# A float32 gated linear-attention block on one core: the split of a reloaded weight tile put late in the key/value stage, and an early gate/up quarter moved to other PSUM banks with the last key/value product ordered behind it

## The chip, the core and the metric

The kernel runs on one core of a Trainium2 chip. A core has five engines with a queue of their own each: TensorE (PE in the profile, PEld for its weight loads), VectorE (DVE), ScalarE (ACT), GpSimd (POOL) and SyncE (SP), which here only issues DMAs. Each engine takes its instructions in the order in which the program lists them, and waits at an instruction until the semaphores that it names have been raised. The metric is device time in microseconds of one execution; the comparison is between medians of repeated executions.

## The reference, cut to what matters

```python
xn = _layernorm(x)                       # x: 1 x 2048 x 576
qkv = xn @ wqkv                          # 32 heads of 18
phi_k = [softmax(k @ w_phi), softmax(-k @ w_phi)]     # per head, 36 features
kv = einsum("bhsf,bhsd->bhfd", phi_k, v)
z  = einsum("bhsf->bhf", phi_k)
o  = (phi_q @ kv) / (phi_q @ z + 1e-6)   # phi_q made of q as phi_k of k
s  = o @ wo
g  = silu((silu(xn @ w_gate) * (xn @ w_up)) @ w_down) # hidden width 4608
out = x + s * g
```

The sums `kv` and `z` run over all 2048 rows, so no row's attention output can be formed before the last key/value row is added.

## The kernel before, in words

All of it is float32. A product in the fast format of TensorE (float32r) is made of three: each operand is split into a rounded part `hi` (a cast on ACT) and the rest `lo` (a subtraction on DVE or POOL), and hi·hi, hi·lo and lo·hi are added in PSUM. `split_rows` (L61) is such a split for a weight tile of the gated branch: one cast on ACT (L62) and two subtractions on DVE (L63, L64).

The program is written with a tile framework. It gives every tile a buffer of its pool, places the waits, and puts the instructions in an order of its own; blocks under `tc.high_priority()` come first among what is ready, and `tc.issue_after(ins)` puts those instructions of a block that run on `ins`'s engine behind `ins` in that engine's queue, and leaves the block's other engines alone.

The stages in order of time:

1. Until about 71 us the rows are normalized, transposed and split (`XB`), weights of keys, queries and values are split, and early tiles of the gated branch run between. An early tile (`early_tile`, L111) is one of the first `EARLY` = 6 blocks of 128 hidden columns of gate and up, made for one half of the rows (`i`) and one block of 512 rows (`j`): 14 matmuls into a gate bank `pg`, Silu on ACT (L117), 14 matmuls into an up bank `pu`, their product on DVE (L120), stored to DRAM. Its weights come from `early_weights(f)` (L99): two tiles `raw` by DMA (L105), each split into `wh` and `wl`. `raw` has two buffers, `wh` and `wl` three. The tiles of f = 0 and f = 1 run for one half of the rows here; for the other half the weights of f = 0 are loaded a second time (L621), and those of f = 1 are kept.
2. From about 71 to 240 us, the key/value stage: eight pairs of 128-row tiles. `k_tile` (L398) makes the keys' features: 28 matmuls into the two-bank PSUM tile `p2` (shown as `p`), per-head maximum and minimum and their subtraction on DVE (L275, L276), Exp on ACT (L279), the sums, reciprocal and scaling on DVE (L282, L283, L406). The values go to the banks `vx`, `vy`, `vw`: two plain products a tile in the first two pairs, and from the third pair on seven products for two tiles (a Strassen-like scheme), whose operands `shi` and `slo` are sums of rows that POOL makes a pair ahead (L308 to L325, the cast of L323 on ACT). Values are copied to the tiles `v0`, `v1` by ACT (L391) or added by DVE (L396). `kv_step` (L286) then adds phi^T·v of one tile into the three banks `kvp`, ten products, for one tile while the next tile is made; the step of the last tile, `kv_step(*pend)` (L486), stands after the loop. In the trace each of the ten is two passes, so a `kv_step` shows 20 matmuls: eight for `kvp0`, eight for `kvp1`, four for `kvp2`.
3. After the loop a quarter of an early tile (f = 1, i = 0, j = 0) runs in the bank pair `p2` (L485), and the sums are turned around: `z` is copied (`zc`, L497), spread over all partitions by small matmuls (L503) and copied to `zb` (L506); each block of `kv` is masked (`km`, L510, DVE) and split (`KVH`, `KVL`).
4. From 240 to about 555 us the queries, their features, the numerators and the projection with `wo` (`WOH`, `WOL`, loaded by L528 through one buffer `ez`), with the other early tiles between.
5. From 555 us to the end the other 30 hidden blocks of gate and up, and the product with `w_down`.

The change touches `early_weights`, `early_tile`, `xw` (which issues the 14 matmuls, L92), the loop of pairs, what stands behind it, and L621.

Of the kernel before, what the change touches and what calls it, by code (L numbers as in the profile page):

```python
# [9 lines left out]
F32 = mybir.dt.float32  # L10
# [6 lines left out]
S, D, H, DH, F = 2048, 576, 32, 18, 4608  # L17
P = 128
NT = S // P
BT = 512  # L20
# [5 lines left out]
GW = GH * DH  # L26
# [20 lines left out]
def gated_hedgehog_kernel(ctx: ExitStack, tc, x, w_qk, w_v, w_phi, wo, w_gu, w_tail, w_down, ident_in, mask_in, out):  # L47
# [5 lines left out]
    nc = tc.nc  # L53
# [7 lines left out]
    def split_rows(hi, lo, src):  # L61
        nc.scalar.copy(hi, src)  # L62
        nc.vector.tensor_sub(lo, src[:, :, 0:2], hi[:, :, 0:2])  # L63
        nc.vector.tensor_sub(hi[64:96, :, 2], src[64:96, :, 2], hi[64:96, :, 2])  # L64
# [17 lines left out]
    def xw(ps, i, j, cols, wh, wl, stationary_x):  # L82
        pairs = []
        for k in range(2):
            b = XB[i][2 * j + k]
            for c in range(2):
                pairs += [(b[:, c, cols], w[:, k, c]) for w in (wh, wl)]
                pairs += [(b[:, 3 + c, cols], wh[:, k, c])]
            pairs += [(b[0:96, 2, cols], wh[0:96, k, 2])]
        for n, (a, b) in enumerate(pairs):  # L90
            l, r = (a, b) if stationary_x else (b, a)
            nc.tensor.matmul(ps, l, r, start=n == 0, stop=n == len(pairs) - 1)  # L92

    est = ctx.enter_context(ExitStack())
    epool = est.enter_context(tc.tile_pool(name="epool", bufs=2, side="right"))
    pes = ctx.enter_context(ExitStack())
    eps = pes.enter_context(tc.tile_pool(name="eps", bufs=2, space=PSUM, side="right"))

    def early_weights(f):  # L99
        parts = []  # L100
        for m in (0, 2):
            raw = epool.tile([P, 2, 3, P], F32, name="raw", bufs=2)
            hi = epool.tile([P, 2, 3, P], F32R, name="wh", bufs=3)
            lo = epool.tile([P, 2, 2, P], F32R, name="wl", bufs=3)
            nc.sync.dma_start(raw, w_gu[f, :, m:m + 2])  # L105
            with tc.high_priority():
                split_rows(hi, lo, raw)
            parts.append((hi, lo))
        return parts

    def early_tile(f, i, parts, js=(0, 1), banks=None):  # L111
        for j in js:
            pg, pu = banks or [eps.tile([P, BT], F32, name="pe") for _ in range(2)]
            xw(pg, i, j, slice(0, BT), *parts[0], False)
            h = epool.tile([P, BT], F32, name="h")
            with tc.high_priority():
                nc.scalar.activation(h, pg, AF.Silu)  # L117
            xw(pu, i, j, slice(0, BT), *parts[1], False)
            with tc.high_priority():
                nc.vector.tensor_mul(h, pu, h)  # L120
            nc.sync.dma_start(h_dram[i, f, :, j * BT:(j + 1) * BT], h)

    with ExitStack() as att:
        const = att.enter_context(tc.tile_pool(name="const", bufs=1))
# [8 lines left out]
        with ExitStack() as wst:  # L133
# [259 lines left out]
            def v_add(v, ps):  # L393
                with tc.high_priority():
                    for d, src in v_parts(v, ps, 0):
                        nc.vector.tensor_add(d, src, d)  # L396

            def k_tile(t):  # L398
# [7 lines left out]
                nc.vector.tensor_mul(heads(phi), heads(phi), spread(sm, 2 * H))  # L406
                return phi

            bank = [0]
# [15 lines left out]
            for p in range(8):  # L425
# [59 lines left out]
            early_tile(1, 0, first_weights[1], (0,), [spare[:, n] for n in range(2)])  # L485
            kv_step(*pend)  # L486

        with ExitStack():
            qc = att.enter_context(tc.tile_pool(name="qc", bufs=1, reuse_waits="tile"))
# [7 lines left out]
                    nc.scalar.copy(zc[0:w, 4 * i + j:4 * i + j + 1], kvp[i][0:w, j, w:w + 1])  # L497
            for a, m in ((0, 4), (4, 1)):
                o, w = GROUPS[a]
                for s in range(2):  # L500
                    zp = kps.tile([P, 512], F32, name=("vx", "vy")[s] if a == 0 else ("vw", "p2")[s])
                    for g in range(a, a + m):
                        nc.tensor.matmul(zp[:, (g - a) * GW:(g - a) * GW + w],  # L503
                                         zc[0:w, 2 * g + s:2 * g + s + 1].to_broadcast([w, P]), ident[0:w, 0:w],
                                         start=True, stop=True)
                    nc.scalar.copy(zb[:, s * D + o:s * D + o + m * w], zp[:, 0:m * w])  # L506
            for i in range(2 * NG):
                o, w = GROUPS[i // 2]
                km = qc.tile([GW, GW], F32, name="km", bufs=2)
# [549 lines left out]
```

## Time and profile before

| | us |
|---|---|
| median of 3 runs (lowest, highest) | 1649.32 (1647.87, 1653.42) |
| the profiled execution | 1654.06 |
| its span, first to last instruction | 1652.2 |
| PE busy | 1611.5 (98%) |
| DVE busy | 1179.7 (71%) |
| ACT busy | 726.7 (44%) |
| POOL busy | 657.0 (40%) |

The views used below: a table of stretches gives the busy time of each engine between two times, and the clock that TensorE was granted (1.00 is full); a timeline lists instructions by their start, with their duration, and in brackets the idle time of the engine before them and what ended it; the chain of waits follows the work that ended last back from the end, here in order of time with start and duration. All times count from the first instruction. A TensorE matmul's shown duration includes its way through the array, so matmuls in a row start closer together than they last.

### The profile page before, as it was taken

The numbers are of one execution on the slowest core, as the hardware profiler recorded it, in microseconds if no ns is written. First come the engines' busy times: TensorE is split into PE (matmuls) and PEld (weight loads), VectorE is DVE, ScalarE is ACT, GpSimd is POOL, SyncE is SP. The second block draws the span as 40 slices with busy tenths as digits, with TensorE's granted clock in tenths as the row PEclk, the third lists the DMA queues.
The fourth block names the chain that finished last, engine by engine and source line by source line (L and its number), as shares of the span: only waits on it lengthen the run. The fifth ranks groups of instructions, "written<-read, shape, count | busy, mean of one in ns | idle before, by whom it ended". The sixth has DMA issues, their size and how long they took to land.

```text
span 1652.2 us, 25252 instructions
## 1 busy us (share of the span) xinstructions
PE 1611.5 (98%) x9399; PEld 1434.4 (87%) x9399; DVE 1179.7 (71%) x1731; ACT 726.7 (44%) x1407; POOL 657.0 (40%) x695
## 2 busy tenths in 40 slices
PE   6989999999999999999999999999999999999997
PEld 5889988899987788888888888888888888888886
DVE  7667767988972376887887777844666677566578
ACT  5533345444452365444445445445433333333334
POOL 3476662233302354554564453422333244133132
PEclk9999999999999999999999999999999999999999
DMA  8522234244317645455455554495545556555434
GB/s 286 200 88 78 77 117 130 79 127 122 90 50 247 236 167 173 170 175 185 160 180 177 174 177 164 134 361 174 167 123 161 174 168 214 155 183 184 139 114 172
DMA packets 121276, 266.46 MB, mean 161 GB/s; under 512 B 12770, under 2 KB 52834, under 8 KB 119362
## 3 DMA queue, kind: packets, MB, share of 16 engines
q1 hardware_dynamic: 106188, 244.49, 45.0%
q0 software_dynamic: 3072, 11.02, 2.5%
q10 hardware_dynamic: 11894, 9.35, 1.8%
q8 instruction: 74, 1.21, 0.3%
q14 instruction: 48, 0.39, 0.1%
HBM read 165.98 MB, written 98.83 MB: 160 GB/s over the span
## 4 chain that ended last, share of the span: by engine, by line
PE 91%; DVE 3%; DMA 2%; issue 1%; ACT 1%; POOL 1%; SPq 0%; ACTq 0%; POOLq 0%; DVEq 0%
PE pd L787 24%; PE px L688 23%; PE pw L688 11%; PE pe L92 7%; PE p L92 7%; PE py L688 6%; PE p L598 4%; PE kvp L292 2%; PE po L584 2%; PE vx L380 1%; PE pt L578 1%; PE vw L380 1%; PE tp L218 1%; DMA xn<-in_A_x 0%; DVE acc L759 0%
## 5 line engine op out<-in xcount | busy, mean ns | idle before, releaser
L787 PEld LDWEIGHTS pd<-dw,hh 128*128 128x128 f32 x3048 | 431.8, 188 | 25.2 <-DVE dw L59 2.2
L787 PE MATMUL pd<-dw,hh 128*128 128x288 f32 x3048 | 447.8, 297 | 3.2 <-DVE dw L59 1.5
L688 PE MATMUL px<-X,w 128*128 128x512 f32 x1440 | 373.5, 393 | 1.8 <-ACT w L58 1.0
L688 PEld LDWEIGHTS px<-X,w 128*128 128x128 f32 x1440 | 261.4, 188 | 53.2 <-ACT s L717 3.9
L688 PE MATMUL pw<-X,w 128*128 128x512 f32 x720 | 185.6, 393 | 0.0
L688 PEld LDWEIGHTS pw<-X,w 128*128 128x128 f32 x720 | 134.7, 189 | 30.4 <-DVE s L722 0.3
L912 DVE TENSOR_TENSOR acc<-pd,acc 128x576 f32<-128x576 f32 x128 | 96.1, 752 | 80.1 <-PE pd L787 80.0
L722 DVE TENSOR_TENSOR s<-pw,s 128x512 f32<-128x512 f32 x120 | 82.5, 687 | 97.7 <-ACT s L717 86.8
L92 PE MATMUL pe<-X,wh 128*128 128x512 f32 (+1 forms) x460 | 144.6, 399 | 1.9 <-POOL X L200 0.7
L717 ACT COPY s<-px 128x512 f32<-128x512 f32 x120 | 70.3, 586 | 154.8 <-PE px L688 154.7
L58 ACT CAST hh<-ha 128x512 fp32r<-128x512 f32 x140 | 82.7, 619 | 95.6 <-PE pd L787 73.3
L59 DVE TENSOR_TENSOR hh<-ha,hh 128x512 fp32r<-128x512 f32 x140 | 108.6, 801 | 17.3 <-ACT hh L58 15.7
L884 POOL TENSOR_TENSOR hb<-hb 128x512 f32<-128x512 f32 x34 | 45.3, 1332 | 163.1 <-DVE hb L744 162.6
L92 PEld LDWEIGHTS pe<-X,wh 128*128 128x128 f32 (+1 forms) x460 | 84.9, 189 | 19.5 <-POOL X L200 1.1
L59 DVE TENSOR_TENSOR w<-ld,w 128x512 fp32r<-128x512 f32 (+1 forms) x90 | 77.1, 859 | 33.4 <-ACT w L58 32.3
L897 POOL TENSOR_TENSOR ha<-ha 128x512 f32<-128x512 f32 x34 | 52.6, 1564 | 109.3 <-DVE hh L59 109.3
L688 PE MATMUL px<-X,wt 96*128 96x512 f32 x240 | 94.8, 395 | 0.0
L688 PE MATMUL py<-X,w 128*128 128x512 f32 x360 | 94.0, 395 | 0.1
L58 ACT CAST w<-ld 128x512 fp32r<-128x512 f32 (+1 forms) x90 | 49.4, 549 | 85.3 <-POOL ld L678 53.7
L871 POOL TENSOR_TENSOR h<-ha,hb 128x512 f32<-128x512 f32 x34 | 45.5, 1338 | 100.8 <-DVE ha L748 66.6
L729 ACT COPY py<-px 128x512 f32<-128x512 f32 x60 | 34.3, 572 | 98.0 <-PE px L688 81.2
L688 PEld LDWEIGHTS py<-X,w 128*128 128x128 f32 x360 | 64.5, 188 | 11.8 <-ACT py L729 1.0
(254 smaller groups left out, 3250.6 us busy)
## 6 DMA issues: line engine op xcount, KB each, us to landing
w_dram<-w SPq DMA_DIRECT2D x87, 512.0 KB, 3.0
w<-w_dram SPq DMA_DIRECT2D x87, 512.0 KB, 4.3
wt<-t_dram SPq DMA_DIRECT2D x59, 336.0 KB, 3.7
ld<-in_B_w_gu SPq DMA_DIRECT2D x30, 512.0 KB
X<-sum_dram SPq DMA_DIRECT2D x8, 1280.0 KB, 10.0
rt<-in_B_w_down SPq DMA_DIRECT2D x33, 288.0 KB, 2.9
rb<-in_B_w_down SPq DMA_DIRECT2D x33, 288.0 KB, 5.9
w_dram<-w SPq DMA_DIRECT2D x29, 256.0 KB, 2.0
```

What stands on the lines that cost most here:

```text
L58: nc.scalar.copy(hi, src)
L59: nc.vector.tensor_sub(lo, src, hi)
L92: nc.tensor.matmul(ps, l, r, start=n == 0, stop=n == len(pairs) - 1)
L598: nc.tensor.matmul(ps[:, 0:HALF], a[0:w, g, jc], bw[0:w, g, n], start=k == 0, stop=k == 3 * NG - 1)
L688: nc.tensor.matmul(ps, l, r, start=first and n == 0, stop=last and n == len(mm) - 1, skip_group_check=True)
L717: nc.scalar.copy(t, ps)
L722: nc.vector.tensor_add(t, ps, t)
L787: nc.tensor.matmul(ps, l, r, start=first and n == 0 and m == 0, stop=n == len(hs) - 1 and m == 2, skip_group_check=True)
L871: sub(s, g["h"][0][0], g["h"][0][1])
L884: nc.gpsimd.tensor_add(a21, a21, g["h"][1][1])
L897: sub(a12, a12, g["h"][0][0])
L912: nc.vector.tensor_add(a2, pd[:, :, 0:HALF], a2)
```

## The change

Four edits:

- `early_weights` takes a second argument `behind`. Where it is given, the split is ordered behind that instruction. For the second load of f = 0 it is the scaling (L406 before, L411 after) of the thirteenth key tile, which `k_tile` now records in `features`. That scaling runs on DVE, so the two DVE subtractions are moved, and the ACT cast is not.
- In each pair from the third on, the `kv_step` of the pair's first tile is written ahead of the last value product (`x[3]` with weights 6) and its copy.
- The early quarter after the loop goes to the banks `vy` (gate) and `vx` (up) in place of `p2`, and the last `kv_step` is ordered behind its last matmul.
- The spread `z` goes to one two-bank tile `p2` (and `vw` for the last, narrow group) in place of `vx`, `vy`, `vw` and `p2` one by one.

```diff
-    def early_weights(f):
+    def early_weights(f, behind=None):
...
             nc.sync.dma_start(raw, w_gu[f, :, m:m + 2])
-            with tc.high_priority():
-                split_rows(hi, lo, raw)
+            with tc.issue_after(behind.ins) if behind else ExitStack():
+                with tc.high_priority():
+                    split_rows(hi, lo, raw)
...
                 sm = softmax_parts(pk, phi)
-                nc.vector.tensor_mul(heads(phi), heads(phi), spread(sm, 2 * H))
+                features.append(nc.vector.tensor_mul(heads(phi), heads(phi), spread(sm, 2 * H)))
...
                 v_add(v1, vx)
+                kv_step(2 * p, phi0, v0)
                 v_product(vx, x[3], 6, False, True)
                 v_copy(v1, vx, 1)
-                kv_step(2 * p, phi0, v0)
...
-            spare = kps.tile([P, 2, 512], F32, name="p2")
-            early_tile(1, 0, first_weights[1], (0,), [spare[:, n] for n in range(2)])
-            kv_step(*pend)
+            spare = early_tile(1, 0, first_weights[1], (0,), [kps.tile([P, BT], F32, name=n) for n in ("vy", "vx")])
+            with tc.issue_after(spare.ins):
+                kv_step(*pend)
...
             for a, m in ((0, 4), (4, 1)):
                 o, w = GROUPS[a]
+                zp = kps.tile([P, 2, 512 if a == 0 else 256], F32, name="p2" if a == 0 else "vw")
                 for s in range(2):
-                    zp = kps.tile([P, 512], F32, name=("vx", "vy")[s] if a == 0 else ("vw", "p2")[s])
...
-            parts = first_weights.pop() if f == 1 else early_weights(f)
+            parts = first_weights.pop() if f == 1 else early_weights(f, features[12] if f == 0 else None)
```

What the framework makes of it. POOL's instructions stand as before. On SP one load of `raw` (for f = 2) moves from the first pairs to the sixth, behind the moved split, since it takes that split's buffer. Line numbers after are larger by 3 to 5 (L406 is L411, L292 is L295, L380 is L383, L503 is L508).

DVE before, in the first two pairs (`p_860` is the key tile of the second tile, `p_955` of the third; `sm` the sums):

```order
L275 TENSOR_REDUCE m<-p_860 128x32
L276 TENSOR_TENSOR phi<-p_860,m 128x576
L282 TENSOR_REDUCE sm<-phi 128x64
L63 TENSOR_TENSOR wl<-raw,wh 128x512
L64 TENSOR_TENSOR wh<-raw,wh 32x2x128
L283 RECIPROCAL sm<-sm 128x64
L406 TENSOR_TENSOR phi<-phi,sm 128x1152
L275 TENSOR_REDUCE m<-p_955 128x32
```

DVE after, at the same place:

```order
L278 TENSOR_REDUCE m<-p_860 128x32
L279 TENSOR_TENSOR phi<-p_860,m 128x576
L285 TENSOR_REDUCE sm<-phi 128x64
L286 RECIPROCAL sm<-sm 128x64
L411 TENSOR_TENSOR phi<-phi,sm 128x1152
L278 TENSOR_REDUCE m<-p_955 128x32
```

DVE after, in the seventh pair (`p_1921` is the key tile of its first tile, `p_2015` of its second):

```order
L286 RECIPROCAL sm<-sm 128x64
L411 TENSOR_TENSOR phi<-phi,sm 128x1152
L63 TENSOR_TENSOR wl<-raw,wh 128x512
L64 TENSOR_TENSOR wh<-raw,wh 32x2x128
L278 TENSOR_REDUCE m<-p_2015 128x32
```

The two subtractions have left the place between the sums and the reciprocal of the second tile and stand behind the scaling of the thirteenth.

ACT before, at the end of a pair (`v_742` is `v0`, `v_743` is `v1`):

```order
L279 ACTIVATE phi<-phi 128x576
L391 COPY v_743<-vx 128x90
L391 COPY v_743<-vx 128x126
L391 COPY v_743<-vx 128x72
L279 ACTIVATE phi<-phi 128x576
L323 CAST shi<-sraw 128x768 x2
```

ACT after, at the same place:

```order
L282 ACTIVATE phi<-phi 128x576 x2
L394 COPY v_743<-vx 128x90
L394 COPY v_743<-vx 128x126
L394 COPY v_743<-vx 128x72
L326 CAST shi<-sraw 128x768 x2
```

The second Exp now stands ahead of the copies of the pair's last value product, and on PE that product follows all ten `kvp` products of the first tile instead of six of them.

PE before, at the end of the stage, the middle of the early quarter (`p_2305`) and what follows its last matmuls (two pieces):

```order
L92 MATMUL p_2305<-X_61,wh 128x512 x2
L92 MATMUL p_2305<-X_61,wl 128x512
L92 MATMUL p_2305<-X_61,wh 128x512 x2
L292 MATMUL kvp_918<-v_743,phi 126x127 x4
L292 MATMUL kvp_919<-v_743,phi 126x127 x4
L92 MATMUL p_2305<-X_60,wh 128x512
L92 MATMUL p_2305<-X_60,wl 128x512
```

```order
L292 MATMUL kvp_920<-v_743,phi 72x73 x2
L503 MATMUL vx<-ident,zc 128x126 x4
L503 MATMUL vy<-ident,zc 128x126 x4
L503 MATMUL vw<-ident,zc 128x72
L503 MATMUL p_2382<-ident,zc 128x72
L92 MATMUL p_2482<-QH,X_64 128x288
```

PE after, from the end of the early quarter (now in `vy` and `vx`) to the first query tile (`p_2481`):

```order
L92 MATMUL vx<-X_61,wl 128x512
L92 MATMUL vx<-X_61,wh 128x512 x2
L295 MATMUL kvp_918<-v_743,phi 126x127 x4
L295 MATMUL kvp_919<-v_743,phi 126x127 x4
L295 MATMUL kvp_920<-v_743,phi 72x73 x2
L508 MATMUL p_2368<-ident,zc 128x126 x4
L508 MATMUL vw<-ident,zc 128x72
L508 MATMUL p_2368<-ident,zc 128x126 x4
L508 MATMUL vw<-ident,zc 128x72
L92 MATMUL p_2481<-QH,X_64 128x288
```

The last tile's ten products stood between the gate and the up half of the quarter, with the last two behind the up half; now all stand behind the whole quarter. The second group of spread `z` follows the first in the same tile.

More of the change, by code (lines that the diff above doesn't have):

```diff
@@ L91, in xw @@
             l, r = (a, b) if stationary_x else (b, a)
-            nc.tensor.matmul(ps, l, r, start=n == 0, stop=n == len(pairs) - 1)
+            last = nc.tensor.matmul(ps, l, r, start=n == 0, stop=n == len(pairs) - 1)
+        return last
     est = ctx.enter_context(ExitStack())
@@ L117, in early_tile @@
                 nc.scalar.activation(h, pg, AF.Silu)
-            xw(pu, i, j, slice(0, BT), *parts[1], False)
+            last = xw(pu, i, j, slice(0, BT), *parts[1], False)
             with tc.high_priority():
@@ L121, in early_tile @@
             nc.sync.dma_start(h_dram[i, f, :, j * BT:(j + 1) * BT], h)
+        return last
     with ExitStack() as att:
@@ L396, in v_add @@
                         nc.vector.tensor_add(d, src, d)
+            features = []
             def k_tile(t):
@@ L499, in gated_hedgehog_kernel @@
                 o, w = GROUPS[a]
+                zp = kps.tile([P, 2, 512 if a == 0 else 256], F32, name="p2" if a == 0 else "vw")
                 for s in range(2):
-                    zp = kps.tile([P, 512], F32, name=("vx", "vy")[s] if a == 0 else ("vw", "p2")[s])
                     for g in range(a, a + m):
-                        nc.tensor.matmul(zp[:, (g - a) * GW:(g - a) * GW + w],
+                        nc.tensor.matmul(zp[:, s, (g - a) * GW:(g - a) * GW + w],
                                          zc[0:w, 2 * g + s:2 * g + s + 1].to_broadcast([w, P]), ident[0:w, 0:w],
                                          start=True, stop=True)
-                    nc.scalar.copy(zb[:, s * D + o:s * D + o + m * w], zp[:, 0:m * w])
+                    nc.scalar.copy(zb[:, s * D + o:s * D + o + m * w], zp[:, s, 0:m * w])
             for i in range(2 * NG):
```

## The prediction

> **What bounds the kernel now.** I read the page, then the waits of PE, then the chain of waits and the timelines around each place that the change touches.
>
> ```profile
> span 1652.2 us, 25252 instructions
> PE 1611.5 (98%) x9399; PEld 1434.4 (87%) x9399; DVE 1179.7 (71%) x1731; ACT 726.7 (44%) x1407; POOL 657.0 (40%) x695
> ```
>
> PE is busy all but 40.7 us of the span. The change adds no matmul and takes none away, so it can only move PE's idle time and the clock that PE gets. Time won in the key/value stage reaches the end as far as PE stays the engine that is waited for. The profiled execution took 1654.06 us, 1.86 more than its span and 4.74 more than the median of the runs, 1649.32. I work out a difference in the profile's time and take it off the median.
>
> The first place is PE's wait before the second `kv_step`. The chain of waits there (start, duration):
>
> ```profile
> 99.33 4.23 PE kvp L292 x20
> 103.56 2.75 PE vw L92 x14
> 106.31 3.73 PE p L92 x28
> ...
> 111.89 2.02 PE kvp L292 x20
> 113.91 1.92 PE vy L92 x14
> ```
>
> The same 20 passes take 4.23 us here and 2.02 one tile later; 14 value matmuls take 2.75 and 1.92. The waits of PE in this stage, and the stretches, say why:
>
> ```profile
> PE kvp L292 <- DVE phi L406: 5.4, 1, 5.4
> ```
>
> ```profile
> 99.33:103.30 3.97, 3.97 (x20) 3.97 (x21) 3.15 (x5) 1.71 (x4) 3.81 (x6) 0.50 0.47 165
> 221.97:240.00 18.03, 14.30 (x96) 12.41 (x94) 13.80 (x29) 8.90 (x32) 12.38 (x13) 1.00 0.31 103
> 229.00:240.00 11.00, 7.96 (x55) 7.05 (x55) 8.12 (x21) 3.94 (x23) 9.24 (x10) 1.00 0.40 133
> 262.31:268.00 5.69, 5.69 (x30) 5.65 (x31) 2.18 (x3) 2.75 (x4) 0.00 (x0) 0.70 0.31 96
> ```
>
> PE stood idle from 93.93 to 99.33, and then had half the clock (0.50). What held it is in the timelines of DVE, ACT and POOL:
>
> ```profile
> 87.52 1.35 DVE L282 TENSOR_REDUCE sm<-phi 128x64 f32<-128x1152 f32 x1 [1.76 <-ACT phi L279]
> 94.34 0.69 DVE L63 TENSOR_TENSOR wl<-raw,wh 128x512 fp32r<-128x512 f32 x1 [5.47 <-ACT wh L62]
> 95.04 0.92 DVE L64 TENSOR_TENSOR wh<-raw,wh 32x256 fp32r<-32x256 f32 x1
> 96.58 2.60 DVE L406 TENSOR_TENSOR phi<-phi,sm 128x1152 f32<-128x1152 f32 x1
> ```
>
> ```profile
> 86.46 0.44 ACT L391 COPY v<-vw 128x252 f32<-128x252 f32 x2
> ...
> 93.47 0.83 ACT L62 CAST wh<-raw 128x768 fp32r<-128x768 f32 x1 [5.99 <-DMA raw<-in_B_w_gu]
> ...
> 95.71 0.67 ACT L351 CAST TH<-sraw 128x576 fp32r<-128x576 f32 x1 [0.90 <-POOL sraw L348]
> 96.29 0.52 ACT L391 COPY v<-vx 128x90 f32<-128x90 f32 x3
> ```
>
> ```profile
> 93.55 0.80 POOL L347 TENSOR_TENSOR sraw<-sraw 128x288 f32<-128x288 f32 x1
> 94.43 1.25 POOL L348 TENSOR_TENSOR sraw<-sraw 128x288 f32<-128x288 f32 x1
> ```
>
> DVE finished the sums at 88.87 and then stood 5.47 us before the subtraction of the reloaded weights, because ACT's cast waited for their DMA until 93.47. The reciprocal and the scaling of the features, which PE needs, are behind it. ACT was held by the same load, and the rest of the values (`v<-vx`) were copied only at 96.29, behind a cast of `TH` that waited for POOL.
>
> **The change, part by part.**
>
> *The moved split at its old place.* With the two subtractions gone, the reciprocal follows the sums at once: 0.55 us for it and at most 2.60 for the scaling (the slowest row) bring `phi` to about 92.1, ahead of PE's 93.93. But the ACT cast stays where it was, so the second reason remains. Of the ten `kvp` products, the first four use values copied at 86.46 and can run at 93.93 (0.8 of the 2.02 us); the other six wait for `v<-vx`. That copy stood behind the `TH` cast, and this behind POOL's L348, which took 1.25 us beside DVE's subtraction where L347 took 0.80. Without the neighbour I give it 0.80, and `v<-vx` comes 0.45 earlier. PE goes on at 96.2, or at 96.9 if nothing on POOL gets faster and all three copies are awaited. The idle time left is 1.5 to 2.2 us. Six products take 1.2, the value matmuls 1.92, and the next key tile starts between 99.3 and 100.0, before 106.31. That is 6.3 to 7.0 us; I take 6.6, in the middle. The rest of the wait and the half clock are in it about equally: 3.0 are the slow rows (2.21 and 0.83).
>
> Whether PE keeps its clock over the idle time left is open. After 2.13 us of idle (the row of 239.99 below) it stayed at 1.00, after 1.94 (262.31 below) it fell, to a mean of 0.70 over 5.69 us, which is 1.7 us lost. So the low end is 6.3 less 1.7, 4.6. The Trainium skill ("TensorE: Matmul & The Clock Gate", HAM oscillation) asks only that no idle gap exceed about 3.4 us; by that rule the term would stay at 6.6 with no low end. The 1.94 us row contradicts it, and the row decides.
>
> *The moved split at its new place.* It goes ahead of the seventh pair's second key tile, where DVE waits:
>
> ```profile
> 201.94 0.76 DVE L275 TENSOR_REDUCE m<-p 128x32 f32<-128x576 f32 x1 [1.88 <-PE p L92]
> ```
>
> 0.69 and 0.92 us fit into 1.88, so it costs nothing; were the cover gone, `m` would be 1.6 us late, and the key tile behind it with its bank. The DMA of `raw` that SP now issues behind it has nothing in its queue behind it until the sums of that pair are stored, and its first reader is in the next stage. No cost.
>
> *The pair.* PE's work is the same, but the last value product ends later by the four `kvp` products ahead of it, and on ACT the copies, then the casts of the row sums for POOL, follow it. A pair before, the first two rows from the chain:
>
> ```profile
> 186.82 0.94 PE vx L380 x7
> 187.76 0.88 PE kvp L292 x8
> ```
>
> ```profile
> 187.79 0.52 ACT L391 COPY v<-vx 128x90 f32<-128x90 f32 x3 [1.70 <-PE vx L380]
> 188.19 0.71 ACT L279 ACTIVATE phi<-phi 128x576 f32<-128x576 f32 x1
> 188.78 1.58 ACT L323 CAST shi<-sraw 128x768 fp32r<-128x768 f32 x2
> ```
>
> ```profile
> 191.93 1.72 POOL L324 TENSOR_TENSOR shi<-sraw,shi 32x256 fp32r<-32x256 f32 x1
> 193.73 1.29 POOL L325 TENSOR_TENSOR slo<-sraw,shi 128x512 fp32r<-128x512 f32 x1
> ```
>
> ```profile
> 195.28 0.29 PE L380 MATMUL vx<-TH,slo 128*128 128x288 f32 x1
> ```
>
> The copies move from 187.79 to 188.67; the Exp is now ahead of them, in time that ACT had idle (1.70), so the casts start at about 189.1 in place of 188.78. POOL's last `slo` then ends near 195.3 in place of 195.02, and PE needs it at 195.28. In five pairs (the fourth to the eighth, which use sums made in such a pair) PE can lose from nothing to 0.3 us each: 0 to 1.7 in all. I take 0.7, nearer the low end since the whole shift is about the slack. There is a second effect on these rows:
>
> ```profile
> 190.91 2.15 DVE L406 TENSOR_TENSOR phi<-phi,sm 128x1152 f32<-128x1152 f32 x1
> ...
> 198.70 1.36 DVE L406 TENSOR_TENSOR phi<-phi,sm 128x1152 f32<-128x1152 f32 x1
> ```
>
> The scaling takes 2.15 beside POOL and 1.36 alone, and POOL's L324 ended just after it: they hold each other up. The Exp half a microsecond earlier puts the scaling against another POOL instruction. The Trainium skill ("SBUF — State Buffer", two separate sides) has VectorE and GpSimd take turns on a shared port pair, each for a whole instruction; by it the scaling gets in ahead of the first `slo` and the last ends near 195.5, some 0.3 a pair, and the term would be 1.4. The rows show the holding up, not the order after the change, so I keep 0.7.
>
> *The end of the stage.*
>
> ```profile
> 229.61 2.00 PE L292 MATMUL kvp<-v,phi 128*126 128x127 f32 x16 [1.29 <-DVE phi L406]
> ...
> 237.45 0.41 PE L503 MATMUL p<-ident,zc 72*128 72x72 f32 x2 [0.30 <-DVE h L120]
> 239.99 0.40 PE L92 MATMUL p<-QH,X 128*128 128x288 f32 x1 [2.13 <-ACT zb L506]
> ```
>
> From 221.97 to 239.99 PE is idle for 1.29, 0.30 and 2.13, 3.72 in all. After, the whole quarter (28 matmuls) hides the last features, so the 1.29 goes; the product on DVE (L120) is long done, so the 0.30 goes. What is late next is the spread of `z`: its second group is written to the same tile as the first, and I read it as waiting until `zb` has been copied from the first, on ACT, behind casts of `KVH` that each wait for a `km` of DVE:
>
> ```profile
> 234.03 0.50 ACT L58 CAST KVH<-km 126x126 fp32r<-126x126 f32 x2 [1.65 <-DVE km L510]
> ```
>
> That cast waited 1.65 once. Bounds for what PE waits there: 0.3, if the `zb` copy passes at once, and 2.2, one such wait and a copy of 0.5. I take 0.7, near the low end, since here DVE isn't stopped by L120 in the middle of its row. Then the query tile follows with no wait for the last copy, as it now takes other banks. Gain 3.7 less 0.7: 3.0 (1.5 to 3.4).
>
> *Behind it.* All this moves PE ahead of the loads of `wo`, which go through one buffer one by one:
>
> ```profile
> 259.23 0.68 ACT L58 CAST WOH<-ez 126x576 fp32r<-126x576 f32 x1 [3.28 <-DMA ez<-in_A_wo]
> ```
>
> ```profile
> 259.94 0.76 DVE L59 TENSOR_TENSOR WOL<-ez,WOH 126x576 fp32r<-126x576 f32 x1 [2.20 <-ACT WOH L58]
> ```
>
> ```profile
> 262.31 0.58 PE L92 MATMUL p<-QH,X 128*128 128x288 f32 x1 [1.94 <-DVE e L276]
> ```
>
> PE waits 1.94 there for a subtraction queued on DVE behind the split of the second block of `wo`. The first load is issued behind POOL's last sums, which depend on ACT's `KVH` casts and not on PE's matmuls, so it moves forward by less than PE. If none of the 3.0 reached the loads, all would be lost here; if they kept pace, nothing. I take a loss of 0.6, near the low end, because each later load is issued by the DVE row behind PE.
>
> *Sum:* 6.6 − 0.7 + 3.0 − 0.6 = 8.3 us less. 1654.06 would become 1645.8, the median 1649.32 becomes 1641.0, 0.5% faster.
>
> **The rivals.**
>
> *The end's gain is lost at `wo`.* For it: the wait exists and DVE is in order. Against: the loads follow PE for most of their way. Then 6.6 − 0.7 = 5.9, less some tenths: about 1643.7.
>
> *The key wait only changes its owner.* ACT's queue, not moved, still holds the values until 96.9, and PE's clock falls all the same: 4.6 of the first term, with the pair and `wo` at their worse ends (1.7, 1.3) and 1.5 at the end: 3.1 us, 1646.2, no difference to be told. For it: the cast of L62 stands where it stood. Against: the copy is at 96.29 already in this trace.
>
> *The clock also stays up at 262.31*, because the windows over which it is judged fall elsewhere: 1.7 more, 1639.3.
>
> *Slower.* The pair's chain PE, ACT, POOL, PE closes on itself, and each pair becomes longer by what POOL is late. It decides from 1.7 us a pair on (8.3 over five); at 2.7 it gives 1654. For it: the slack is only 0.26 (195.28 less 195.02). Against: the product moves by 0.88, so being later than that needs POOL's four instructions to slow down too; L324 at 1.72 against some 0.7 is the largest such stretch.
>
> **How the numbers follow.** Forecast 0.52, end's gain lost 0.18, clock kept at 262.31 as well 0.10, owner changed 0.13, slower 0.07. A difference under 0.3% (4.9 us) can't be told from none. The first and third are faster, and of the second two thirds: 0.75. Within: 0.18. Slower: 0.07. The range runs from 1649.3 − 12.6 (7.0, no loss in the pairs, 3.4, 1.7 at 262.31, and 0.5 for the scatter of the median) to the rival whose owner changed, with a microsecond of scatter: 1636.7 to 1647.2.
>
> **What would show it.** Right: the PE wait for `phi` before the second `kv_step` is gone, with 1 to 2.5 us behind the first four products, ended by ACT's copy (L394); a key tile near 100 in place of 106.31; pairs of 18.2 to 18.5 us; no wait for `phi` at the end, and one of under 1.5 before the second spread of `z`; the first query tile some 9 us earlier than 239.99. Wrong: a pair of 19 us or more, a new half-clock stretch before 100, or a wait above 4 us where 1.94 was.

## The result and the profile after

The changed kernel took 1646.26 us in the median of 14 executions (1644.42 to 1648.05), the kernel before 1650.54 in as many beside it: a ratio of 0.9973, with an interval of 0.9965 to 0.9982, 4.3 us less. In a second comparison it was 1646.18 against 1652.02, 0.9961 (0.9949 to 0.9974), 5.8 us less. The forecast was 8.3 us less, at 1641.0. So the sign was right and the size was not.

The profiled execution took 1644.69. Its page:

```profile
span 1642.9 us, 25249 instructions
PE 1610.5 (98%) x9399; PEld 1433.5 (87%) x9399; DVE 1176.6 (72%) x1731; ACT 727.5 (44%) x1407; POOL 653.2 (40%) x695
```

The waits of PE at the places of the change (total, times, longest):

```profile
PE p L92 <- DVE e L279: 2.7, 1, 2.7
PE p L508 <- ACT zb L511: 0.8, 1, 0.8
PE kvp L295 <- ACT v L394: 0.4, 1, 0.4
```

The waits for `phi` (5.4 and 1.3) are gone. 0.4 is left at the first place and 0.8 before the second spread of `z`, and the wait at the third query tile has grown from 1.94 to 2.7.

*The first place.* ACT's timeline, then the chain of waits:

```profile
92.87 0.84 ACT L62 CAST wh<-raw 128x768 fp32r<-128x768 f32 x1 [5.64 <-DMA raw<-in_B_w_gu]
...
95.15 0.51 ACT L394 COPY v<-vx 128x90 f32<-128x90 f32 x3
```

```profile
93.74 0.81 POOL sraw L351
...
95.43 1.40 PE kvp L295 x12
96.83 1.93 PE vw L92 x14
98.76 3.73 PE p L92 x28
```

ACT still waits for the reloaded weights, but the copies of the values come at 95.15 in place of 96.29, and PE goes on at full clock: the value matmuls take 1.93 in place of 2.75, and the next key tile starts at 98.6 in place of 106.1.

*The new place of the split.* DVE, ahead of the seventh pair's second key tile:

```profile
192.76 1.50 DVE L63 TENSOR_TENSOR wl<-raw,wh 128x512 fp32r<-128x512 f32 x1
194.28 1.14 DVE L64 TENSOR_TENSOR wh<-raw,wh 32x256 fp32r<-32x256 f32 x1
195.45 0.76 DVE L278 TENSOR_REDUCE m<-p 128x32 f32<-128x576 f32 x1
```

The two subtractions took 0.69 and 0.92 at their old place and take 1.50 and 1.14 here, beside POOL's sums: 2.64, more than the 1.88 that should have covered them. The reduction behind them has no idle time left.

*The pair.* DVE's scaling, then POOL's operands for the next pair:

```profile
165.11 1.65 DVE L411 TENSOR_TENSOR phi<-phi,sm 128x1152 f32<-128x1152 f32 x1
```

```profile
164.81 0.73 POOL L327 TENSOR_TENSOR shi<-sraw,shi 32x256 fp32r<-32x256 f32 x1 [4.75 <-ACT shi L326]
165.62 2.28 POOL L328 TENSOR_TENSOR slo<-sraw,shi 128x512 fp32r<-128x512 f32 x1
167.98 0.73 POOL L327 TENSOR_TENSOR shi<-sraw,shi 32x256 fp32r<-32x256 f32 x1
168.79 1.29 POOL L328 TENSOR_TENSOR slo<-sraw,shi 128x512 fp32r<-128x512 f32 x1
```

```profile
169.88 1.19 PE vx L383 x7
```

Before, the scaling (190.91) met the second L324 (1.72), and the first `slo` went ahead of it:

```profile
190.56 1.28 POOL L325 TENSOR_TENSOR slo<-sraw,shi 128x512 fp32r<-128x512 f32 x1
```

Now the scaling starts ahead of the first `slo`, which takes 2.28 in place of 1.28. The last `slo` ends at 170.08, inside PE's `vx` product, which takes 1.19 where seven of its kind take 0.94 elsewhere: 0.25 a pair.

*The end of the stage.* PE:

```profile
225.12 2.18 PE L295 MATMUL kvp<-v,phi 128*126 128x127 f32 x20
...
229.21 1.16 PE L508 MATMUL p<-ident,zc 126*128 126x126 f32 x8 [0.79 <-ACT zb L511]
...
230.34 0.38 PE L92 MATMUL p<-QH,X 128*128 128x288 f32 x1
```

All twenty passes of the last `kv_step` run in one piece, and the only wait left is 0.79, where 0.7 was forecast. The first query tile starts at 230.34 in place of 239.99, 9.65 us earlier.

*The loads of `wo`.* SP before, then after:

```profile
246.11 0.44 SPq L528 DMA_DIRECT2D ez<-in_A_wo  x1
249.21 0.83 SPq L535 DMA_DIRECT2D tl<-in_B_w_tail  x2
250.14 0.36 SPq L105 DMA_DIRECT2D raw<-in_B_w_gu  x1
...
253.25 0.33 SPq L105 DMA_DIRECT2D raw<-in_B_w_gu  x1
254.14 0.34 SPq L528 DMA_DIRECT2D ez<-in_A_wo  x1
```

```profile
239.38 0.44 SPq L533 DMA_DIRECT2D ez<-in_A_wo  x1
242.08 0.83 SPq L540 DMA_DIRECT2D tl<-in_B_w_tail  x2
243.02 0.36 SPq L106 DMA_DIRECT2D raw<-in_B_w_gu  x1
...
243.96 0.38 SPq L106 DMA_DIRECT2D raw<-in_B_w_gu  x1
244.44 0.42 SPq L533 DMA_DIRECT2D ez<-in_A_wo  x1
```

The first load of `wo` moved forward by 6.7 us, less than PE, and the second by 9.7, as PE did. So what stands between them closed up: the second load was issued 4.9 us behind the first load of `tl` before, and 2.4 now, with both loads of `raw` in between. What it then took, before and after (chain of waits, start and duration):

```profile
254.14 5.07 DMA ez<-in_A_wo
```

```profile
244.44 5.82 DMA ez<-in_A_wo
250.29 0.68 ACT WOH L58
```

Until it had landed, the DMA engines moved more than before (the last two figures are their busy share and GB/s; before, then after):

```profile
254.14:259.21 5.07, 5.07 (x30) 4.49 (x29) 3.30 (x4) 0.95 (x1) 4.83 (x11) 1.00 0.74 202
244.44:250.27 5.83, 5.83 (x33) 5.08 (x32) 3.24 (x4) 0.95 (x1) 4.89 (x11) 1.00 0.81 285
```

And the third query tile, which waits for it through DVE, in the table of stretches after:

```profile
253.36:258.84 5.48, 5.48 (x29) 5.48 (x30) 2.02 (x2) 2.75 (x4) 0.00 (x0) 0.69 0.34 105
```

It runs at a mean clock of 0.69 and takes 5.48, where its 28 matmuls take 3.73 at full clock. In the profile before it took 5.50, behind the shorter wait.

### The profile page after: what moved, and what is told of

Read it like the earlier page. It is cut to its first block, busy times and chain, and to the rows that moved or that the text cites. A ratio compares the mean times of both kernels' runs of the same rounds, so it can differ in the third digit from the quotient of the medians.

```text
span 1642.9 us, 25249 instructions
## 1 busy us (share of the span) xinstructions
PE 1610.5 (98%) x9399; PEld 1433.5 (87%) x9399; DVE 1176.6 (72%) x1731; ACT 727.5 (44%) x1407; POOL 653.2 (40%) x695
## 4 chain that ended last, share of the span: by engine, by line
PE 92%; DMA 3%; DVE 2%; POOL 1%; ACT 1%; issue 1%; ACTq 0%; SPq 0%; POOLq 0%; DVEq 0%
PE pd L792 25%; PE px L693 24%; PE pw L693 11%; PE pe L92 7%; PE p L92 6%; PE py L693 6%; PE p L603 4%; PE po L589 2%; PE kvp L295 2%; PE vx L383 1%; PE pt L583 1%; PE vw L383 1%; DMA sraw<-in_A_w_v 1%; PE tp L221 1%; PE tp L193 0%
## 5 line engine op out<-in xcount | busy, mean ns | idle before, releaser
L680 POOL TENSOR_TENSOR ts<-ld 128x256 f32<-128x256 f32 x30 | 27.2, 908 | 120.8 <-issue 69.3
```

## The experiments

**Each part alone, and the kernel before again.** The profiled executions of before and after differ by 9.4 us, the medians by 4.3. So the first question was whether the parts are worth what the traces show.

> The kernel before, unchanged, as a second profile of it. Theory A (the steps are worth what the two profiles show, 9.3 us, and the profile of before was a slow execution, by the places of TensorE's half-clock stretches, which come at other times in each execution): its time is near the median, 1650.5, the key tile after the second key/value step starts 1 to 2 us earlier than 106.1 since the half clock holds for 3.4 us in place of 6.8, and 1 to 2 us more are won where another half-clock stretch is missing. Theory B (the steps are as large in every execution, and the changed kernel gives about 5 us back at another place in most executions, but not in the one profiled): the stretches of this profile are as in the first one within 0.5 us up to 300 us.

> The kernel before with the moved split alone; PE's, ACT's and POOL's order are those of before. Theory A: the fourth key tile starts near 98.6, 7.5 us earlier in the profile, but 4 to 6 us in the median, less what the later wait for the second block of wo takes back: median 1645 to 1646.5, as fast as all edits together. Theory B: 1642.5 to 1643.5, since neither the pairs nor the end are touched.

> The kernel before with the early quarter in vy and vx, the last key/value step behind it and z spread in p2 and vw; the split and the pairs as before. Theory A and the profiles: the first query tile starts 3.4 us earlier relative to the eighth pair, and 0.7 to 3 us of it are lost at the wait for the second block of wo: 1647.5 to 1650. Theory B: 1647 with no loss behind it.

> The changed kernel with the pair written as before: the key/value step of the first tile behind the last value product. If the pairs cost what the profile shows (18.46 us a pair in place of 18.20, five to six times): pairs of 18.2 us and 1.3 to 1.6 us less than the changed kernel, 1644.7. If the gain in the pairs is taken back at the wait for wo: pairs of 18.2 us, and the changed kernel's time.

The edits, each of the changed kernel's diff: `split_only` has `behind` and `features` alone; `end_only` the quarter in `vy` and `vx`, the last `kv_step` behind it and `z` in `p2`; `after_old_pairs` is the changed kernel with

```diff
-                kv_step(2 * p, phi0, v0)
                 v_product(vx, x[3], 6, False, True)
                 v_copy(v1, vx, 1)
+                kv_step(2 * p, phi0, v0)
```

| on one chip, before 1651.87 (30 executions) | median us | ratio, interval |
|---|---|---|
| before again | 1651.33 | 0.9995 (0.9985 to 1.0004) |
| split alone | 1647.59 | 0.9972 (0.9962 to 0.9983) |
| end alone | 1650.13 | 0.9988 (0.9977 to 0.9999) |
| all but the pairs' order | 1646.10 | 0.9964 (0.9951 to 0.9977) |

The split alone brings 4.3 of the 5.8 us, the end alone 1.7, and both without the new order of the pairs 5.8. Wherever the split is moved, the first place works in the trace (key tile four 9.9 to 10.2 us behind key tile three, against 16.6 to 18.0), and where it stands alone the key tiles show its price at the new place: from the fourteenth to the fifteenth 9.39 us in place of 8.66. I had costed that at nothing. Both forecasts for the split alone, 1645 to 1646.5 and 1642.5 to 1643.5, were too low. The end saves 3.2 us up to the first query tile, and its median shows half of that. Where the rest goes is in the traces of the end alone and of the split alone, at the third query tile:

```profile
260.62 0.37 PE L92 MATMUL p<-QH,X 128*128 128x288 f32 x1 [3.19 <-DVE e L278]
```

```profile
255.27 0.37 PE L92 MATMUL p<-QH,X 128*128 128x288 f32 x1 [0.27 <-DVE e L277]
```

From the first query tile to the fourth, the end alone takes 2.6 us more than the mean of the kernel before, and the split alone as much as that mean. So the new end of the stage brings the loss at `wo`, and the moved split does not. Without the new order, the pairs take 18.20 us in the trace in place of 18.46, as expected, but the time, 0.9964 of before, can't be told from the changed kernel's 0.9961 and 0.9973: the price of the pairs is seen in the traces only. As to the two theories: the kernel before run again has the same 6.83 us at half clock in its trace (A has no support there), and the parts add up to less than their traces, so something is given back, as B has it, though not 5 us.

**Is the idle time, or the clock, other in most executions than in the profiled ones?** Idle products on PE (written to a bank that is overwritten next) fill the first wait of the kernel before without moving anything else:

```diff
+                            if p == 1 and j == 0:
+                                warm = kps.tile([P, 512], F32, name="vw")
+                                for _ in range(30):
+                                    nc.tensor.matmul(warm[:, 0:HALF], XB[0][0][:, 0, 0:P], KVWH[:, 0, 0, 0:HALF],
+                                                     start=True, stop=True)
                             kv_step(*pend)
```

> The kernel before, with 30 idle products put on TensorE ahead of the second kv_step (into the bank vw, overwritten by the value product that follows). At 0.137 us each (14 value matmuls took 1.92) they last 4.1 us and lie in the wait of 5.40, of which 1.3 stays, so nothing moves but the clock: the 20 kvp passes take about 2.0 in place of 4.23, the value matmuls 1.92 in place of 2.75, and the fourth key tile comes near 103.1 in place of 106.1. Theory 'windows' (the traces are right on the idle time, and part of the half clock that a removed wait saves comes back as half-clock windows of 3.41 us elsewhere): 1.3 to 2.5 us faster than before, mean clock 0.001 higher. Theory 'all of it' (the slow rows cost 3.0 in every execution and nothing comes back): 3.0 us faster, mean clock 0.002 higher. Theory 'short wait' (in most executions the reloaded weights land earlier than in the profiled ones and the wait is nearer 3 us): no faster than before, or up to 1 us slower, though the trace shows the clock kept.

> The changed kernel itself, beside the kernel before on one chip with the other three. By the steps of the traces so far it should stand to the version with the moved split alone as: end 3.3 less, pairs 1.3 more, 0.6 less at the fourteenth key tile, about 1 more at the loads of wo, so some 1.5 us below it: 6 us below the kernel before (0.9963). If part of the half clock comes back elsewhere: 4 to 5.5 us below. Its trace: key tile four 10.1 behind key tile three.

> The kernel before with 30 idle products in the first wait, once more, beside the version with 60 of them. If the clock is what the idle products buy: again about 6 us below the kernel before (0.996 to 0.997), mean clock 0.998 or more in most executions, against 0.995 of the kernel before. If the first result was chance: 1.5 to 3 us below it. Fourth key tile 13.9 us behind the third.

> The same with 60 idle products, 8.2 us in place of 4.1, so that they outlast the wait. With the clock kept in both, the difference of the two times is 8.2 less the wait that executions really have. If it is as long as in the profiles (5.40 in that of the kernel before): 2.8 us slower than with 30, and the fourth key tile 16.6 behind the third. If the wait of most executions is short (3 us): 4.1 slower, since then the 30 already outlast it.

With 30 products the chain (here of the second comparison) shows `kvp` and the value matmuls without the half clock behind the wait, and with 60 the products take its place:

```profile
101.62 2.28 PE kvp L292 x20
103.90 1.92 PE vw L92 x14
```

```profile
93.88 7.91 PE vw L438 x60
101.79 2.02 PE kvp L292 x20
```

30 products: 1645.75 (5 executions, 0.9967, 0.9954 to 0.9979) and, in a second comparison, 1647.92 (12, 0.9978, 0.9964 to 0.9992), 4 to 6 us less than before, though PE only does more work. 60 products, which outlast the wait by 2.5 us: 1651.35, 0.9999 (0.9988 to 1.001), no slower than before. With a gain of 4 to 6 us, "short wait", which had none, falls. The two versions lie 3.4 us apart in the medians, and in their traces the fourth key tile comes 13.89 and 17.42 us behind the third, 3.5 apart. Both intervals are some 2 us wide to each side, so this distance can't tell the 2.8 of a long wait from the 4.1 of a short one.

The mean granted clock is a second measure. Over 68 executions of the kernel before it is 0.9952, over 23 of the changed kernel 0.9963, over 16 with 30 products 0.9978 (one execution left out, told of at the end), over 12 with 60 products 0.9973. Of a span of 1650 us, 0.001 is 1.65 us of work. Filling the wait wins about 4.2 us of clock, taking the wait away only 1.8. So some of the half clock comes back in the changed kernel, as "windows" has it; on the products themselves "windows" (1.3 to 2.5 us) and "all of it" (3.0) both put too little. The loads of `wo` are not the only place. The split alone, with no wait there to speak of, has 0.9964 over ten executions, no more than the changed kernel: its trace has 3.41 us of half clock from 232.93, at the first query tile, behind a wait of 2.13. The three traces with products have such a stretch at that tile too, behind 2.06 and 2.07.

**Where does it come back?** Four more traces of the changed kernel and two of the kernel before.

> The changed kernel, a further profiled execution. If the half clock that the first wait no longer costs comes back at the loads of wo: a stretch of 3.41 or 6.83 us at half clock near 253 us, with a wait of 2.5 to 3.5 us before the third query tile. If it is scattered: such stretches at other places, and none near 253 in most of these executions.

> The same as the run before it: a half-clock stretch near 253 us behind a wait of 2.5 to 3.5 us, or none there and others elsewhere.

> The same as the two runs before it. From the traces of the changed kernel together: stretches near 253 in four or more of six if the loads of wo are the place, in two or fewer if it is scattered.

> The same once more: a half-clock stretch near 253 us behind a wait of 2.5 to 3.5 us, or none there and others elsewhere.

> The kernel before, a further profiled execution. From the third key tile to the fourth 16.5 to 18 us, as in the three traces so far that have the old place of the split (17.95, 16.56, 17.21), with 6.83 us at half clock, if those are typical. If most executions are shorter there, as the difference of the medians (4.3 to 5.9) against that of the traces (6.5 by their parts) would have it: 14 to 16 us, or one stretch of 3.41 only.

> The same once more: 16.5 to 18 us between the third and the fourth key tile with 6.83 us at half clock, or 14 to 16 us with 3.41.

All six traces of the changed kernel have a stretch at half clock near 253 us (3.41 us in five, 6.83 in one), behind waits of 2.7 to 4.1 us for the second load of `wo`. That load took 5.8 to 6.8 us in all six, and 3.2 to 5.1 in the four of the kernel before, where PE waited 0.3 to 1.9 and one trace of four had half clock there. The longest, in the third of the new traces, chain and PE:

```profile
245.20 6.84 DMA ez<-in_A_wo
```

```profile
255.13 0.37 PE L92 MATMUL p<-QH,X 128*128 128x288 f32 x1 [4.11 <-DVE e L279]
```

All four traces of the kernel before have 6.83 us at half clock at the first place, and the two new ones 16.14 and 16.94 us from the third key tile to the fourth, so the profiled one (17.95) was at the long end there, but of the same kind. With these, the time between landmarks on PE, as means of four and six executions:

| from, to | before | after | difference | forecast |
|---|---|---|---|---|
| start, fourth key tile | 106.29 | 98.86 | −7.4 | −6.6 |
| fourth to sixteenth key tile | 109.97 | 111.34 | +1.4 | +0.7 |
| sixteenth key tile, first query tile | 23.38 | 20.45 | −2.9 | −3.0 |
| first query tile, first gate/up block behind the queries | 305.73 | 308.42 | +2.7 | +0.6 |
| from there to the end of the span | 1105.26 | 1105.24 | 0.0 | 0 |
| sum | 1650.63 | 1644.32 | −6.3 | −8.3 |

All of the 2.7 us of the fourth row are lost between the first query tile and the fourth; from there to the gate/up block the two kernels take the same time to about 0.1 us.

**Against the two prices.**

> The changed kernel with the order of the pairs as before (kv_step behind the last value product), but for the seventh pair, beside which the moved split stands. With the old order in all pairs the fourteenth key tile took 9.40 us (split at 2.65 us on DVE, 0.7 more than its cover), with the new order in all pairs 8.84, while the new order costs 0.27 in each other pair. Expected: 9.53 and 8.7 to 8.9 us in the seventh pair, 0.5 us less than the changed kernel with all old pairs, 1.1 less than the changed kernel. If the pairs' price depends on the pair before: within 0.3 us of the old pairs.

> The same, with the rows of wo loaded into the four buffers of the query features (e) instead of one buffer of their own (ez), so that up to four loads run at once. The scheduler then orders the first query tiles anew. If the wait for the loads is what holds the third query tile (2.7 us in the profile of the changed kernel, and the half clock behind it, 1.7 in some executions): 2 to 4 us less than pair7. If another wait takes its place in the new order: within 1 us of it, or slower.

> The changed kernel with the old order of the pairs, and the two moved subtractions in two places: the first behind the scaling of the eleventh key tile, the second behind that of the thirteenth. Beside POOL's sums they took 1.51 and 1.14 us on DVE; together they outlast the wait of 1.88 of DVE, each alone fits. Expected: the step from the fourteenth key tile to the fifteenth 8.67 in place of 9.40, 0.7 us less than the changed kernel with old pairs, 6.5 us below the kernel before. If the wait isn't 1.88 at the eleventh tile: 9.4 there instead, and no gain.

> The same, with the second block of wo loaded into a buffer of e, its subtraction ordered on DVE behind the last subtraction of the second query tile, and the other three blocks loaded after that tile in the program. The third query tile then doesn't wait behind a DMA on DVE. If the wait of 2.7 to 3.4 us there, and the half clock behind it, is where the changed kernel gives back part of its gain: 2 to 4 us less than with two places alone, mean clock 0.001 to 0.002 higher. If the scheduler's new order of the query tiles makes other waits, as with four buffers: within 1 us, or slower.

`pair7` (the new order `if p == 6` only): 1646.15, 0.9965 (0.9952 to 0.9978). The expectation missed: the fourteenth step stays at 9.47, so the new order doesn't hide the split when it stands in that pair alone, and the fifteenth rises to 9.68. Why it does when all pairs have it (8.84) I did not settle. With the rows of `wo` in four buffers of `e`,

```diff
-                wr = qk.tile([P, 2 * D], F32, name="ez", bufs=1)
+                wr = qk.tile([P, 2 * D], F32, name="e", bufs=4)
```

it became 1648.16, 0.9977 (0.9967 to 0.9986): the scheduler ordered the first query tiles anew, and PE waits 3.8 us at the same bank and 3.1 for a Silu:

```profile
PE p L92 <- DVE e L279: 3.8, 1, 3.8
PE pe L92 <- ACT h L119: 3.1, 2, 1.8
```

`two_places` has the old order of the pairs and one subtraction behind each of two scalings, those of the eleventh and the thirteenth key tile (`features[10]`, `features[12]`):

```diff
+                    nc.scalar.copy(hi, raw)
+                    with tc.issue_after(behind[0].ins):
+                        nc.vector.tensor_sub(lo, raw[:, :, 0:2], hi[:, :, 0:2])
+                    with tc.issue_after(behind[1].ins):
+                        nc.vector.tensor_sub(hi[64:96, :, 2], raw[64:96, :, 2], hi[64:96, :, 2])
```

DVE there, at the sixth and at the seventh pair:

```profile
175.09 1.51 DVE L111 TENSOR_TENSOR wl<-raw,wh 128x512 fp32r<-128x512 f32 x1
177.06 0.76 DVE L285 TENSOR_REDUCE m<-p 128x32 f32<-128x576 f32 x1 [0.45 <-PE p L92]
```

```profile
193.41 1.13 DVE L113 TENSOR_TENSOR wh<-raw,wh 32x256 fp32r<-32x256 f32 x1
195.26 0.76 DVE L285 TENSOR_REDUCE m<-p 128x32 f32<-128x576 f32 x1 [0.72 <-PE p L92]
```

Each subtraction leaves idle time behind it, all the steps are 8.67 and 9.53 again, and the time is 1644.75, 0.9957 (0.9943 to 0.9971), 7.1 us below the kernel before. `two_places_wo` also takes the second block of `wo` out of DVE's way: it loads that block into a buffer of `e`, orders its subtraction behind those of the second query tile, and loads the other three blocks after that tile. It took 1643.97, 0.9955 (0.9939 to 0.9970). The wait at the third query tile is gone, but in the new order PE waits for Silu (1.6) and for a projection's bank (1.4), and the mean clock of its seven executions is 0.9966, no higher than the 0.9973 of the six of `two_places`. So it isn't shown that this wait can be taken away at a profit. Both versions are faster than the kernel before. Against the changed kernel their intervals overlap. The changed kernel's four new traced executions, on the same chip, took 1645.20 to 1648.17, their median 1.4 above `two_places`; with so few executions the lead of one to two microseconds isn't proven.

## Why the prediction was wrong in size

*First wait, 6.6 forecast.* The place and the order of events were right, and the size was 0.8 too small: 7.4. `phi` is no longer waited for, and the copies of the values came at 95.15, ahead of the 95.84 to 96.3 that I had worked out, because POOL's last sum ended at 94.55 (93.74 and 0.81) where it had ended at 95.68: 1.1 us earlier, not the 0.45 that I gave it. Those 0.45 came as forecast (0.81 in place of 1.25); the other 0.7 is a load that POOL's sums waited for in both profiles and that landed earlier in the second, which I had not looked at. The idle time left is 0.3 to 0.8 us in six traces, not 1.5 to 2.2. The fear that the clock falls again at this place did not come true. One thing I had not seen: the fourth key tile of the kernel before lies at 106.1 to 106.6 in all four traces, wherever the third starts (88.2 to 90.4); a late arrival is absorbed by the wait, and the gain shrinks by as much.

*Moved split at no cost.* Wrong: "0.69 and 0.92 us fit into 1.88". The durations were taken from another place. Beside POOL's sums it was 2.65 us, and 0.7 us were lost where the split was moved alone. In the changed kernel only 0.1 to 0.2 of that is seen; what it loses is the next term.

*Pairs, 0.7 forecast.* 1.4 for the whole stretch, 0.25 to 0.28 a pair. The Trainium skill ("SBUF — State Buffer", two separate sides) has the shared port pair held for a whole instruction, and by that I had worked out 0.3 a pair and 1.4 in all, with VectorE's scaling getting in ahead of the first `slo`. The trace agrees: the `slo` that starts half a microsecond behind the scaling takes 2.28 in place of 1.28. I had that value in hand and kept the lower one, since the order after the change could not be read from the rows; the direction of the shift was enough to read it.

*End of the stage, 3.0.* Right: 2.9, with a wait of 0.79 where I gave 0.7.

*The loads of `wo`, 0.6 forecast.* This is the step that failed: "near the low end, because each later load is issued by the DVE row behind PE". The second load did keep up with PE: it moved forward by 9.7 us, as the first query tile did. But the first load moved by 6.7 only. I had written that it moves by less, since it stands behind POOL's last sums, and gave that no price. In all traces it is issued 6.1 us behind the first query tile with the old end of the stage and 8.9 to 9.6 behind it with the new one, so nearly nothing of the end's gain reached it. The loads in front of the second one closed up, from between 4.8 and 8.0 us to between 2.4 and 2.8, and the same transfer took longer. PE's wait went from 0.3 to 1.9 up to 2.7 to 4.1, and with it the half clock came in every trace. 2.7 us in place of 0.6 is about all that the forecast had too much by its own parts, as the errors at the first place and in the pairs nearly cancel. That the new end brings this loss is shown by the end alone and the split alone. That the transfer takes longer because of the loads closed up in front of it is read from the traces, and in all that load `wo` through `ez` it is so (3.2 to 5.1 us with the old end, 5.8 to 6.8 with the new one); no run spaced the loads apart to test it.

*The rivals.* "The end's gain is lost at `wo`" (1643.7, chance 0.18) was nearer the truth: 2.9 won and 2.7 lost. Its reason, loads that don't follow PE, holds for the first load and not for the second. "The key wait only changes its owner" named 1646.2, almost the measured time, by luck: what it describes did not happen, since the wait left is 0.3 to 0.8 us and the clock stays up behind it. For the same reason it says nothing for the working that the measured time lies in the range, which reaches up to that rival.

*The base.* The median of three from which I subtracted, 1649.32, was 1.2 below that of fourteen, so the 1641.0 was too low by as much from the start. The parts give 6.3 in the traces; the medians give 4.3 in one comparison (by its interval 3.0 to 5.8) and 5.8 in the other (4.3 to 8.4). I cannot attribute the distance between 6.3 and 4.3: four and six traces stand for executions that scatter by 4 to 8 us.

*The clock.* The row was the better guide than the rule. The Trainium skill ("TensorE: Matmul & The Clock Gate", HAM oscillation) asks only that no gap exceed some 3.4 us, and in the traces the clock fell behind waits of 2.7, 3.1 and 3.2 at the third query tile. Yet after 2.5 at the same place in the trace of `two_places` it did not. And 2.13 us of idle before the first query tile kept the clock in the profile of the kernel before, and lost it in that of the split alone. The length alone doesn't decide.

## What to carry to other kernels

A stall of TensorE can cost more than its idle time: behind the waits of 4.0 to 5.4 us at the first place the clock was halved for 6.83 us in all five traces that have them. 30 products that compute nothing, put into a wait that cannot be removed, took as much off this kernel as the change did. When a stage is moved forward, look at each of its transfers for what issues it, and at what it is now issued next to: here the first load of `wo` did not follow, the second did, and arrived late all the same, behind loads that stood closer together. And take the duration of a moved instruction from beside the neighbours it will have, not from the place it leaves.

## What was not expected of the hardware

In all twenty traces, half clock comes in stretches that are whole multiples of 3.41 us (but for the one in which the execution ends) and lie a whole number of such steps behind the first rise of the clock (98.45 − 16.53 is 24 of them in the profile of the kernel before). That two waits of the same length differ in price, as the two of 2.13 us do, fits this; where in such a step a wait must lie to cost the clock was not worked out.

One profiled execution with 30 products was granted 0.95 in place of 1.00 nearly throughout, and yet did the same work in the same stretch. That execution, then the kernel before (from 300 to 1600 us):

```profile
300.00:1600.00 1300.00, 1294.65 (x7281) 1141.06 (x7281) 917.99 (x1331) 569.58 (x1102) 487.32 (x505) 0.95 0.52 167
```

```profile
300.00:1600.00 1300.00, 1294.61 (x7286) 1141.10 (x7285) 918.69 (x1331) 568.97 (x1102) 488.87 (x505) 1.00 0.52 167
```

It took 1649.3 us, where the four others of that set took 1645.45 to 1648.29, so in this one execution 5% less granted clock went with at most 0.3% more time. Stretches at 0.50, in contrast, made the same twenty passes take 4.23 us in place of 2.02.
